# Attention and GELU layer on one core: reordered work between the first softmax and the first output blocks

**Chip, cores, metric.** One core of a Trainium2 chip (trn2). The metric is device time in microseconds (us) of one execution; the span of a profile is some 1.8 us shorter than it.

## The reference

```python
qn = q / (norm(q, axis=1) + 1e-6);  kn = k / (norm(k, axis=1) + 1e-6)   # 4 batches, 6080 x 256
a  = softmax(kn.T @ qn / tau)                                            # 256 x 256 per batch
x  = (v @ a).reshape(24320, 256)
h  = x @ w_in;  out = gelu_tanh(h) @ w_out                               # 256 -> 2048 -> 256
```

The kernel folds `a @ w_in` into one matrix `aw` per batch (256 x 2048), so that a block of 512 rows of v needs only two large products: `hp = aw.T @ v.T`, a gelu on ScalarE (ACT), and `yp = g.T @ w_out`.

## The kernel before

For batch 0, q and k come in ten chunks; each is cast (DVE), squared (ACT), and put into the Gram matrix G and the column sums (TensorE, "PE"). Then comes the softmax of batch 0, then 48 v blocks, in whose gaps the next batch's Gram matrix is computed. SyncE (SP) issues plain stores and DMA transposes; GpSimd (POOL) issues the loads that cast to bf16.

```python
# last chunks of batch 0: q squared by DVE, k by ACT
if n >= n_chunks - 2:
    nc.scalar.activation(sqb[:, 1, lo:hi], st[:, 1, lo:hi], AF.Square)
    nc.vector.tensor_mul(sqb[:, 0, lo:hi], qkb[:, 0, lo:hi], qkb[:, 0, lo:hi])
...
# GpSimd's loads, in this order: first weights in four parts, v block 1, second weights,
# first q/k chunk of batch 1, v block 2
for fs in range(D // 512):
    nc.gpsimd.dma_start(out=win_bf[:, :, fs * 512 : fs * 512 + 512], in_=...)
load_v(1)
for half in range(2):
    nc.gpsimd.dma_start(out=wout_bf[:, half * 8 : half * 8 + 8, :], in_=...)
load_qk(1, 0)
load_v(2)
# softmax of batch 0
nc.scalar.activation(r, cols[:, 0:4], AF.Sqrt)
norms(r)                      # DVE: r + eps, then reciprocal
Gs = scaled(G, r)
keep_clock(5)                 # needless matmuls
T = turned(Gs)                # PE
... exp -> eT; v block 0 turned on PE; row_sums(eT); first products aw = eT.T @ w_in
...
# main loop, per block: DMA transposes of v two blocks ahead, load three blocks ahead
vT = vT_of.pop(nb)
turn_v(nb + 2)                # four dma_start_transpose on SyncE
load_v(nb + 3)
...
# while blocks 0 and 1 run: further loads of batch 1 (n counts the steps)
for n in range(10):
    if n % 5 == 0 and (b, n // 5) not in loaded_of:
        load_qk(b, n // 5)    # the second q/k chunk, at n == 5
    if b == 1 and n == 5:
        turn_v_on_pe(1)
    yield
```

## Time and profile before

| | before |
|---|---|
| time, median of the first 3 runs | 757.6 us (757.37 to 758.07) |
| profiled run | 757.1 us, span 755.3 |
| PE busy | 98% |
| first hp of block 0 / of block 2 | 41.52 us / 67.00 us |
| lost by PE at block 2's first hp | 0.54 us |

The profile's lines are in the prediction. How to read them: after 70 us PE never waits, so the end is set by the moment at which it starts on v block 2. The wait for block 2's turned v just before that is called the door here. Note that the profiled run, 757.1 us, lies at the quick end of the kernel's own spread.

### The profile page before, as it was taken

How to read it: one execution, taken by the hardware profiler on the slowest of the kernel's cores; microseconds unless marked ns; L12 is line 12 of the kernel's file. 1: busy time of each engine (PE TensorE's matmuls, PEld its weight loads, DVE VectorE, ACT ScalarE, POOL GpSimd, SP SyncE). 2: the span in 40 equal slices, each digit the busy share in tenths (PEclk: the TensorE clock that was granted, in tenths of full speed). 3: DMA queues.
4: the chain of work that ended last, by engine and by line, in shares of the span. 5: the costliest groups of instructions: out<-in, count | busy, mean ns of one | idle time of the engine just before them, and what ended most of it. 6: DMA issues, size and time to landing. Idle time of an engine off the chain costs nothing.

```text
span 755.3 us, 12358 instructions
## 1 busy us (share of the span) xinstructions
PE 738.0 (98%) x5272; PEld 504.6 (67%) x5272; DVE 278.3 (37%) x485; ACT 420.3 (56%) x412; POOL 70.0 (9%) x127
## 2 busy tenths in 40 slices
PE   4899999999999999999999999999999999999998
PEld 3556666667666666666666666666767666666666
DVE  3645545454402545553421455454441011011011
ACT  5775555556455555555555555555545655555552
POOL 0231010001021111001031000100101000000000
PEclk9999999999999999999999999999999999999999
DMA  9999957115149678313449385621512633322111
GB/s 351 357 194 180 189 87 154 53 43 83 43 103 214 133 133 137 65 43 66 101 94 221 80 130 101 125 80 47 82 43 78 111 79 76 69 74 53 41 57 56
DMA packets 80759, 83.59 MB, mean 111 GB/s; under 512 B 55488, under 2 KB 60224, under 8 KB 80704
## 3 DMA queue, kind: packets, MB, share of 16 engines
q0 software_dynamic: 17648, 32.97, 27.0%
q1 hardware_dynamic: 62752, 48.98, 24.6%
q8 instruction: 41, 0.67, 0.4%
q10 hardware_dynamic: 304, 0.85, 0.3%
q14 instruction: 14, 0.11, 0.1%
HBM read 78.91 MB, written 24.90 MB: 137 GB/s over the span
## 4 chain that ended last, share of the span: by engine, by line
PE 95%; DMA 3%; DVE 0%; ACT 0%; SPq 0%; issue 0%; DVEq 0%
PE yp L463 44%; PE hp L536 44%; PE G L141 5%; DMA st<-in_k_dram 3%; PE ps L201 2%; PE cols L153 1%; PE T L179 0%; PE yp L567 0%; PE idle L137 0%; SPq L80 0%; DVE qkb L242 0%; ACT g L540 0%; PE ps L348 0%; ACT eT L328 0%; DVE Gs L171 0%
## 5 line engine op out<-in xcount | busy, mean ns | idle before, releaser
L540 ACT ACTIVATE g<-hp 128x1024 bf16<-128x1024 f32 (+1 forms) x384 | 389.8, 1015 | 308.6 <-PE hp L536 308.5
L463 PE MATMUL yp<-wout_bf,g 128*128 128x256 bf16 x3024 | 392.0, 273 | 0.0
L536 PE MATMUL hp<-vT,aw 128*128 128x512 bf16 (+1 forms) x1536 | 390.8, 377 | 0.4 <-ACT g L540 0.4
L463 PEld LDWEIGHTS <-g 128*128 128x128 bf16 x3024 | 295.9, 98 | 113.4
L536 PEld LDWEIGHTS <-aw 128*128 128x128 bf16 x1536 | 149.9, 98 | 105.0 <-issue 1.3
L480 DVE COPY ysb<-yp 128x512 f32<-128x512 f32 (+1 forms) x95 | 64.9, 683 | 403.1 <-PE yp L463 403.1
L404 DVE TENSOR_TENSOR acc<-acc,sq 128x512 f32<-128x512 f32 (+1 forms) x141 | 97.5, 692 | 4.8
L141 PE MATMUL G<-qkb 128*128 128x256 bf16 (+1 forms) x384 | 69.8, 282 | 12.8 <-DVE qkb L242 12.8
L403 DVE TENSOR_TENSOR sq<-qkb 128x512 bf16<-128x512 bf16 (+1 forms) x141 | 58.7, 417 | 0.0
L141 PEld LDWEIGHTS <-qkb 128*128 128x128 bf16 (+1 forms) x384 | 37.8, 101 | 21.5 <-DVE qkb L242 15.0
L280 POOL DMA_DIRECT2D vb<-in_v_dram x47 | 25.5, 544 | 142.7 <-DMA vT<-vb 122.8
L210 DVE TENSOR_SCALAR aw<-ps,rsinv 128x512 bf16<-128x512 f32 x30 | 22.4, 749 | 27.0 <-PE ps L201 26.7
L247 ACT ACTIVATE sqb<-st 128x3072 bf16<-128x3072 f32 (+3 forms) x9 | 20.4, 2287 | 11.6 <-DMA st<-in_k_dram 11.6
L80 POOL DMA_DIRECT2D qkb<-in_q_dram x24 | 13.0, 542 | 148.7 <-PE hp L536 82.4
L242 DVE CAST qkb<-st 128x3072 bf16<-128x3072 f32 (+4 forms) x11 | 14.5, 1326 | 15.4 <-DMA st<-in_k_dram 15.3
L201 PE MATMUL ps<-win_bf,eT 128*128 128x512 bf16 x60 | 17.7, 379 | 0.0
L414 POOL TENSOR_TENSOR r<-r,half 128x4 f32<-128x4 f32 x3 | 3.1, 1044 | 141.7 <-DVE r L413 141.7
L80 POOL DMA_DIRECT2D qkb<-in_k_dram x24 | 13.1, 544 | 4.1 <-DMA qkb<-in_q_dram 2.3
L520 POOL COPY g<-gr 128x1024 bf16<-128x1024 bf16 x2 | 2.1, 1040 | 105.3 <-PE yp L463 105.3
L439 DVE RECIPROCAL den<-den 128x256 f32<-128x256 f32 x6 | 10.5, 1753 | 0.2
L554 POOL COPY gr<-g 128x1024 bf16<-128x1024 bf16 x2 | 2.1, 1036 | 87.6 <-ACT g L540 87.6
L137 PE MATMUL idle<-filler 128*128 128x512 bf16 x36 | 9.5, 391 | 0.0
(65 smaller groups left out, 85.1 us busy)
## 6 DMA issues: line engine op xcount, KB each, us to landing
out_dram<-ysb SPq DMA_DIRECT2D x44, 512.0 KB, 2.9
vb<-in_v_dram POOLq DMA_DIRECT2D x43, 256.0 KB, 8.6
qkb<-in_q_dram POOLq DMA_DIRECT2D x21, 384.0 KB, 6.6
qkb<-in_k_dram POOLq DMA_DIRECT2D x21, 384.0 KB, 8.7
st<-in_q_dram SPq DMA_DIRECT2D x5, 768.0 KB, 9.5
st<-in_k_dram SPq DMA_DIRECT2D x4, 768.0 KB, 11.3
vT<-vb SPq DMA_TRANSPOSE x184, 3.5
out_dram<-ysb SPq DMA_DIRECT2D x4, 384.0 KB, 4.0
```

What stands on the lines that cost most here:

```text
L80: engines[x].dma_start(out=dst[:, x, 0:size, :], in_=src[b, s0 * 128 : (s0 + size) * 128, :].rearrange("(p s) c -> p s c", s=size))
L141: nc.tensor.matmul(G[:, ic, :], lhsT=qk[:rows, 1, s, ic * 128 : ic * 128 + 128], rhs=qk[:rows, 0, s, :], start=first and ic == 0, stop=las ...
L201: nc.tensor.matmul(ps, lhsT=eT[:, jc, ic * 128 : ic * 128 + 128], rhs=win_bf[:, jc, fs * 512 : fs * 512 + 512], start=jc == 0, stop=jc == 1)
L210: nc.vector.tensor_scalar_mul(dst, ps, scale)
L247: nc.scalar.activation(sqb[:rows, :, lo:hi], st[:rows, :, lo:hi], AF.Square)
L280: nc.gpsimd.dma_start(out=t[:, 0:n, :], in_=v_rows[r0 : r0 + n * 128, :].rearrange("(p s) c -> p s c", s=n))
L403: nc.vector.tensor_mul(sq[:rows], flat, flat)
L404: nc.vector.tensor_add(acc[:rows], acc[:rows], sq[:rows])
L463: nc.tensor.matmul(yp[:rows, at, :], lhsT=g[:, fc, s * 128 : s * 128 + rows], rhs=wout_bf[:, fc, :], start=fc == 0, stop=fc == FC - 1)
L480: nc.vector.tensor_copy(ysb[:, s0 : s + 1, :], yp[:, 0 : s + 1 - s0, :])
L536: nc.tensor.matmul(hp[:, j, :cols], lhsT=aw[:, cc, fc * 128 : fc * 128 + 128], rhs=vT[:, cc, :cols], start=cc == 0, stop=cc == 1)
L540: nc.scalar.activation(g[:, 2 * i : 2 * i + 2, :cols], hp[:, :, :cols], AF.Gelu_apprx_tanh)
```

## The change

Its intent: shorten the softmax chain and have v block 2 on the core earlier. The core of the diff:

```diff
-            if n >= n_chunks - 2:
+            if n == n_chunks - 2:            # last chunk: both squares on ACT
...
-    for fs in range(D // 512):
+    for c0, c1 in ((0, 512), (512, 1024), (1024, D)):     # three weight loads
...
+    load_v(2)
     load_qk(1, 0)
-    load_v(2)
...
-    keep_clock(5)
+    (v block 0 turned on PE here: eight transposes into two PSUM tiles)
+    keep_clock(1, pY, "y")
     T = turned(Gs)
+    keep_clock(1, pY, "y")
+    nc.vector.tensor_copy(vT0[:, 0, :], vps[0])
...
+    first_aw(0, 0); first_aw(1, 0)       # products of the first half of eT
     rsinv = row_sums(eT)
+    first_aw(0, 1); first_aw(1, 1); ...  # then of the second half
```

## The prediction

> **What bounds the kernel now.** I read the page first: busy shares, then the chain of work that ended last, to learn which engine's time is the kernel's time.
>
> ```profile
> PE 738.0 (98%) x5272; PEld 504.6 (67%) x5272; DVE 278.3 (37%) x485; ACT 420.3 (56%) x412; POOL 70.0 (9%) x127
> ...
> PE 95%; DMA 3%; DVE 0%; ACT 0%; SPq 0%; issue 0%; DVEq 0%
> ```
>
> TensorE is the kernel: 95% of the chain, 98% busy. A change in another engine's work is worth only the time that it lets TensorE start earlier or wait less. The whole span is 755.3 us and the device time 757.6 us. I then cut the span into stretches, to see where TensorE is not yet full.
>
> ```profile
> 0.00:27.50 27.50, 16.59 (x131) 10.13 (x131) 12.18 (x13) 15.40 (x8) 1.46 (x8) 1.00 0.95 369
> 27.50:36.40 8.90, 6.98 (x106) 5.64 (x107) 7.82 (x9) 7.63 (x5) 3.68 (x6) 1.00 0.97 338
> 36.40:41.60 5.20, 4.63 (x42) 2.96 (x40) 3.30 (x9) 3.53 (x7) 3.93 (x6) 1.00 1.13 153
> ...
> 65.00:70.00 5.00, 4.62 (x30) 2.54 (x29) 3.45 (x7) 2.34 (x3) 2.60 (x5) 1.00 0.87 175
> 70.00:755.00 685.00, 681.75 (x4821) 469.29 (x4819) 241.41 (x433) 374.92 (x373) 54.03 (x96) 1.00 0.47 93
> ```
>
> The columns are stretch, length, busy time of PE, weight loads, DVE, ACT, POOL, then clock, DMA share and GB/s. Up to 36.4 us the kernel waits for the first batch's q and k, which the change does not touch. From 36.4 to 41.6 lies the softmax of the first batch, where filler matmuls inflate the busy time: it is a chain of engines. After 70 us TensorE is full, so whatever is gained before it should reach the end undiminished. One hole is left, in 65 to 70. So the change can act in two places only. The chain in order of time shows the first.
>
> ```profile
> 36.85 0.31 PE cols L153 x8
> ...
> 37.19 0.18 ACT r L320
> ...
> 37.40 0.43 DVE r L164
> ...
> 38.14 0.49 DVE Gs L171
> ...
> 38.77 0.75 PE T L179 x4
> ...
> 39.54 0.85 ACT eT L328 x2
> ...
> 40.44 0.23 PE rs L188 x3
> 40.66 0.90 PE ps L348 x8
> 41.56 1.00 PE hp L536 x4
> ```
>
> Column sums, root, norms, scaled Gram matrix, its turn, two exponentials, row sums, products: 4.7 us with no slack drawn. The turning of v block 0 is not in this list. The chain calls the products (ps) the last link before hp; the timeline of DVE says it less simply:
>
> ```profile
> 39.98 0.69 DVE L337 CAST vT<-vps 128x512 bf16<-128x512 f32 x1 [0.97 <-PE vps L333]
> 40.70 0.17 DVE L194 RECIPROCAL rsinv<-rs 128x2 f32<-128x2 f32 x1
> 40.98 1.28 DVE L357 TENSOR_SCALAR aw<-ps,rsinv 128x256 bf16<-128x256 f32 x3
> ```
>
> The first aw eviction needs the product and the reciprocal. The reciprocal ends at 40.87 and the eviction starts 0.11 us later, the same gap as between the norms' reciprocal (37.85 + 0.19 = 38.04) and Gs (38.14) in the chain. The row sums end at 40.67, so the reciprocal was as early as it could be.
>
> The second place is the hole:
>
> ```profile
> 66.24 0.38 PE L141 MATMUL G<-qkb 128*128 128x256 bf16 x2
> 66.44 0.69 DVE L480 COPY ysb<-yp 128x512 f32<-128x512 f32 x1 [4.21 <-PE yp L463]
> 66.97 0.34 PEld L536 LDWEIGHTS <-aw 128*128 128x128 bf16 x3 [0.63 <-issue]
> 67.00 0.59 PE L536 MATMUL hp<-vT,aw 128*128 128x512 bf16 x2 [0.38 <-ACT g L540]
> ```
>
> Counting eight hp groups per block from 41.5 us, 67.00 is the first hp of v block 2. The profile names a gelu, but this hp reuses the buffer of the gelu that ended at 65.29, and no other block start of the run has that wait. What is special is block 2's turned v: it comes by DMA transposes that SyncE can issue only once v block 2 has landed (its wait ends at 55.15). The fourth was issued at 59.40; the medians of landing over short stretches put its landing at 7.4 us later, 66.8. Then hp starts. G's two matmuls would have let it start at 66.24 + 2 x 0.11 = 66.46, so the loss is 0.54 us.
>
> **What the Trainium skill says.** (1) "DMA: Bandwidth & Descriptors", section "Issuing engines are not separate DMA queues": transfers of all issuing engines run on the same 16 DMA engines and interleave. The trace agrees: the first transpose, beside the q/k loads, took 8.4 us to land, against a median of 3.5 us over the run. So order within the loads is the only lever. (2) "ScalarE: Activation LUTs", "What ACT_TABLE_LOAD costs": an ACTIVATE with immediates takes 186 ns + 0.833 ns per element, a table load 1283 ns. The trace has 0.61 to 0.63 us at 512 elements (formula 0.61), 1.91 at 2048 (1.89), and 1.28 for the load. (3) "TensorE: Matmul & The Clock Gate", "Part 4: PE-mode transpose": transposes do not count as busy for the clock gate as matmuls do. The trace before has 1.6 us of transposes almost unbroken (38.77 to 40.38) at clock 1.00, so it does not show the danger.
>
> **The change, part by part.**
>
> Last chunk's squares: before, ACT squares k (35.43 to 36.06) while DVE casts (to 36.18) and then squares q (36.32 to 36.74), and the column sums' weight loads wait until 36.80. Now ACT does both in one instruction of 1024 elements: 0.19 + 0.85 = 1.04 us, ending at 36.47. The last Gram matmul starts at 36.58 and holds the array 0.11, so the sums start at about 36.70 instead of 36.80. Gain 0.10 us, on the chain.
>
> v block 0 turned early: eight transposes (about 1.04 us in all) move to 37.0 to 38.1, where four of five fillers go away (4 x 0.215 us). v landed at 28.87 + 7.7 = 36.6, in time. One filler ends by 38.4, before Gs at 38.63. The DVE copy (0.69) falls from 39.0 to 39.7, when DVE was idle. In the kernel before, this work lay beside the exponentials and off the chain: it just missed delaying the reciprocal (40.67 against the row sums' 40.67). Gain 0.
>
> Products at the first exponential: two of eight matmuls (0.22 us) move before the row sums. The first product ends 0.11 us sooner, the second 0.22. But the first eviction is still held by the row sums, the reciprocal and the 0.11 us gap; the second, on ACT, starts about 0.12 us sooner, but hp's second matmul would not run before its first has streamed for 0.215. Gain 0, at most 0.1.
>
> v block 2's load ahead of the chunk: the landings before, as issue plus time to landing, are wout's second half 37.82 + 12.5 = 50.3, the chunk's q 52.0, k 53.5, v block 2 55.1. It moves to right behind wout. 256 KB at the 0.2 MB per us of that stretch is 1.3 us, so it lands near 51.6, 3.5 us earlier. Its transposes follow: the fourth at about 63.3, 3 us before it is wanted. Gain 0.54 us. The chunk lands 1.3 us later, near 55.2; its first Gram matmul is at 57.67. Free.
>
> First weights in three loads, not four: they are in place as before, except that columns 1024 to 1535 now wait for the whole last half. Its landing was 35.65 + 8.2 = 43.85. Its first reader (third group of ps) ran at 44.12 and would now run at 44.0. Free by 0.15 us.
>
> Sum: 0.10 + 0 + 0 + 0.54 = 0.64 us, and 757.6 - 0.64 is 756.96. With half of the possible 0.1 from the products I say 756.9.
>
> **Rivals.** (a) The big weight load becomes the wait: if it lands 0.5 us late, the first 0.1 and more is lost, though an earlier start of POOL's next descriptors (one issue of about 0.75 us fewer) speaks against. The gain from block 2 stays or is merged: 757.3. (b) Block 2's hole was another wait, the named gelu or the buffer; then it stays, and the time is 757.5. Against it: it happens once among 47 starts. (c) The products at the first exponential do help, as the author meant, if the 0.11 us gap is not a cost of the reciprocal but the product's end (40.91): then 0.1 to 0.2 more, 756.7. The two ends lie within 0.01 us of each other, so I cannot tell them apart. (d) With fewer fillers the clock drops: a few microseconds at half speed would be 2 us lost, 759. Against it: the early transposes fill the same stretch, and the longest pause gets shorter, from 0.5 us to about 0.25. (e) The chunk, later by 1.3 us and beside the earlier transposes, stalls the Gram matmuls: slack is 2.4 us, so it needs twice the delay.
>
> **Range and chances.** The three runs before spread over 0.7 us, more than the effect. With 0.64 as the base, (c) below and (a), (b) above: 756.2 to 757.6. A 2% change would be 15 us; nothing in 34 us to 70 us can give that, and nothing after it changes. Within 2%: 0.98.
>
> **What would show it.** In the profile after: column sums of the last chunk starting 0.1 us sooner after its last load; SyncE's first transposes near 51.6 instead of 55.15; no wait at the first hp of block 2; the distance from the end of the exponentials to the first hp unchanged at 1.13 us (39.54 + 0.85 to 41.52), less if (c) holds; the third ps group without a wait. It would be wrong if the load of the first 36 us itself shifts from run to run, as nothing of that is in my sum, or if ps waits for the wide weight load.

## The result, and the profile after

| | before | after |
|---|---|---|
| median (6 runs each, same rounds) | 757.59 us (757.25 to 758.07) | 757.62 us (757.0 to 758.44) |
| profiled run, span | 755.3 us | 755.9 us |
| last chunk's cast starts | 35.44 us | 35.28 us |
| first hp of block 0 | 41.52 us | 40.98 us |
| PE ready for block 2 | 66.46 us | 66.11 us |
| first hp of block 2 | 67.00 us | 67.52 us |

The ratio is 1.0001, with a 95% interval of 0.9988 to 1.0014. Ratios in this text are the mean time of one kernel's fast runs over that of the other's of the same rounds, so not quite the ratio of the medians. No change clear of the noise, where I had forecast 0.7 us less; the median lies 0.02 us outside my range.

The timeline of the changed kernel through the softmax (columns: start, duration, engine, line, operation, names, shapes; in brackets the idle time before and what ended it):

```profile
36.52 0.34 PE L153 MATMUL cols<-ones_bf,sqb 128*128 128x1 bf16 x8
...
36.90 0.17 ACT L319 ACTIVATE r<-cols 128x4 f32<-128x4 f32 x1 [0.58 <-PE cols L153]
...
37.11 0.17 DVE L164 TENSOR_SCALAR r<-r 128x4 f32<-128x4 f32 x1 [1.12 <-ACT r L319]
...
40.16 0.17 DVE L194 RECIPROCAL rsinv<-rs 128x2 f32<-128x2 f32 x1 [1.09 <-PE rs L188]
...
40.44 1.27 DVE L369 TENSOR_SCALAR aw<-ps,rsinv 128x256 bf16<-128x256 f32 x3
...
43.77 0.10 PEld L201 LDWEIGHTS <-eT 128*128 128x128 bf16 x1 [0.31 <-issue]
```

This stage did better than forecast. From the last chunk's cast to hp it takes 40.98 - 35.28 = 5.70 us, where it took 41.52 - 35.44 = 6.08. Of the 0.38 us, 0.13 is the squares (cast to root: 36.90 - 35.28 = 1.62, was 1.75). The other 0.25 is one DVE instruction that adds epsilon to four columns: 0.17 us here and 0.42 before. The rest is the same to 0.01 us: root to hp less that instruction is 4.08 - 0.17 = 3.91 now and 4.33 - 0.42 = 3.91 before. (A further 0.16 us of the earlier hp is only an earlier last load.) The last line shows a new wait: the weight load of the third product group comes 0.31 us after the one before it, once the wide weight load is in. Without a wait that gap is 0.12 us, so PE lost 0.19: from the first hp to this group it took 43.77 - 40.98 = 2.79 us, against 44.12 - 41.52 = 2.60 in the kernel before.

The chain of waits of the changed kernel from 50 to 70 us, in order of time, is the answer to the hole of before:

```profile
51.56 1.30 SPq L294
...
55.47 11.80 DMA vT<-vb
...
67.52 1.02 PE hp L548 x4
```

v block 2 is on the core at 51.54 us (before: 55.13), as forecast, and its transposes are issued from 51.56 to 55.47. But the fourth takes 11.8 us to land, at 67.28, where I had assumed some 7.4. The timeline of PE in the changed kernel at this door:

```profile
65.89 0.38 PE L141 MATMUL G<-qkb 128*128 128x256 bf16 x2
67.52 1.02 PE L548 MATMUL hp<-vT,aw 128*128 128x512 bf16 x4 [1.25 <-DMA vT<-vb]
```

PE could have gone on at 65.89 + 0.22 = 66.11 and loses 1.41 us, against 0.54 before. It arrives 0.35 us sooner (the 0.54 of the first hp, less the 0.19 of the third group) and leaves 0.52 later; the spans differ by 0.6. Why do transposes that were issued 3.6 us earlier land no earlier? The DMA view has the packets of each queue; q0 carries GpSimd's loads, q1 the transposes. First the kernel before, from 59 to 63 and from 64 to 67 us (columns: packets, MB, share of the 16 engines' time; a line of a single DMA has its size and its us to landing):

```profile
q0 software_dynamic: 300, 0.75, 96.0%
q1 hardware_dynamic: 295, 0.07, 13.8%
...
q1 hardware_dynamic: 1742, 0.40, 134.8%
q0 software_dynamic: 25, 0.05, 8.9%
```

Then the changed kernel, from 55 to 64 and from 64 to 68 us:

```profile
q0 software_dynamic: 647, 1.64, 97.5%
q1 hardware_dynamic: 593, 0.14, 12.0%
...
qkb<-in_k_dram POOLq DMA_DIRECT2D x1, 384.0 KB, 11.7
...
q1 hardware_dynamic: 1727, 0.45, 117.6%
q0 software_dynamic: 58, 0.13, 16.1%
```

As long as loads are queued, each queue gets one packet in turn: 295 against 300, 593 against 647. But a load's packet carries 0.75 MB / 300 = 2.5 KB and a transpose's 0.07 / 295 = 0.24 KB. So the transposes crawl at 70 packets per us. When the loads thin out, from about 64 us, they go at several hundred per us. The last load queued beside them (the k half of the third q/k chunk, issued at 54.98, the qkb line above) lands at 66.7; block 2's four transposes land at 60.9, 64.7, 66.9 and 67.3. In the kernel before, that load lands at 65.8 and the four at 63.6, 66.1, 66.4 and 66.8. The landing is set by the end of the load queue, not by the issue. The Trainium skill has this rule, "DMA: Bandwidth & Descriptors", section "Queues, rings and completion order": each DMA engine round-robins between its queue rows at packet granularity. The equal counts agree with it; whether the trace's packets are that page's packets, no run here shows. I had quoted another section of that page and not drawn this conclusion.

### The profile page after: what moved, and what is told of

The parts are those of the page before. It is cut to its first block, busy times and chain, and to the rows that moved or that the text cites. A ratio compares the mean times of both kernels' runs of the same rounds, so it can differ in the third digit from the quotient of the medians.

```text
span 755.9 us, 12264 instructions
## 1 busy us (share of the span) xinstructions
PE 731.4 (97%) x5183; PEld 503.5 (67%) x5269; DVE 277.6 (37%) x484; ACT 420.6 (56%) x412; POOL 69.2 (9%) x126
## 4 chain that ended last, share of the span: by engine, by line
PE 90%; issue 5%; DMA 3%; POOL 1%; SPq 0%; ACT 0%; DVE 0%; POOLq 0%; ACTq 0%
PE yp L475 43%; PE hp L548 41%; PE G L141 4%; DMA vb<-in_v_dram 2%; DMA vT<-vb 2%; PE ps L201 1%; SPq L294 0%; POOL win_bf L309 0%; PE cols L153 0%; PE yp L579 0%; POOL wout_bf L312 0%; PE T L179 0%; ACT g L552 0%; POOL vb L280 0%; POOL filler L117 0%
## 5 line engine op out<-in xcount | busy, mean ns | idle before, releaser
L548 PE MATMUL hp<-vT,aw 128*128 128x512 bf16 (+1 forms) x1457 | 385.0, 377 | 5.4 <-DMA vT<-vb 1.3
L247 ACT ACTIVATE sqb<-st 128x3072 bf16<-128x3072 f32 (+4 forms) x10 | 21.4, 2163 | 11.7 <-DMA st<-in_k_dram 9.3
```

Source lines behind the costliest of these rows:

```text
L247: nc.scalar.activation(sqb[:rows, :, lo:hi], st[:rows, :, lo:hi], AF.Square)
L548: nc.tensor.matmul(hp[:, j, :cols], lhsT=aw[:, cc, fc * 128 : fc * 128 + 128], rhs=vT[:, cc, :cols], start=cc == 0, stop=cc == 1)
```

## Experiments

**Theory (queue).** The door at block 2 opens when GpSimd's loads run dry; nothing that PE or the load order of v block 2 gains before it gets past it. **Rivals.** (1) A transpose simply takes 9 to 12 us on this path. (2) There is no door: PE is the bound from 41 us on. (3) The wide weight load ate the gain. There were twelve experiments, all with correct results, five timed runs each, in three sessions; the kernel before ran in each session (medians 757.26, 757.30, 757.47). All edits move or add work only. All verdicts by the 2% rule are "same"; intervals are given where they matter.

### Holding the loads back

```diff
         for n in range(10):
+            if b == 1 and n == 5:     # reads the four turned slices of block 2, so it waits for them
+                nc.gpsimd.tensor_copy(gate2, vT_of[2][0:1, 0, :])
             if n % 5 == 0 and (b, n // 5) not in loaded_of:
                 load_qk(b, n // 5)
```

> The changed kernel, with one small GpSimd copy that reads the four turned slices of v block 2, put before the load of the second q/k chunk, so that no further q/k load is queued beside these transposes. Queue theory (the transposes get one small packet for each large packet of the software loads and land only when those loads run dry): the fourth transpose lands near 58 instead of 67.3, the wait at block 2's first hp (1.25 us) is gone, and the time falls by about 1.3 us, to 756.3. Rival (a transpose simply takes 9 to 12 us from its issue on this queue, whatever else is queued): the fourth still lands near 67, the wait stays at about 1.2 us, time 757.6.

Measured: 756.23 us median (755.98 to 757.79), ratio to before 0.9988 (0.9976 to 1.0001). The slow one, 757.79, has a mean clock of 0.998 (see the end). The timeline of GpSimd in this kernel shows when the last transpose was in:

```profile
59.57 1.08 POOL L398 COPY gate<-vT 1x512 bf16<-1x512 bf16 x1 [13.71 <-DMA vT<-vb]
```

So 59.4 us rather than 67.3. I had said 58; the fourth was issued at 55.53 and took 3.8 us. PE has no wait at all after 42 us. Rival (1) is out.

The same copy went into the kernel before.

> The same copy in the kernel before, where v block 2 lands at 55.1. Queue theory: its transposes land near 60 to 61, the wait at block 2 (0.54 us lost) is gone, the time falls by 0.5 to 757.1. Rival (fixed latency of a transpose): no change, 757.6, wait 0.4.

Measured: 756.46 us (756.26 to 756.84), ratio 0.9988 (0.9974 to 1.0001), and no wait of PE. With no load beside them the four transposes land 2.3 to 2.9 us after their issue, the last at 61.6:

```profile
61.77 0.93 POOL L386 COPY gate<-vT 1x512 bf16<-1x512 bf16 x1 [15.80 <-DMA vT<-vb]
```

The medians differ by 0.80 us, where the profile before had 0.54 to give; the interval holds both, and no gain as well.

As a dose test, the copy was put one chunk later in the changed kernel (`if b == 1 and n == 0` ahead of `load_qk(b, n + 2)`).

> A dose test: the changed kernel with the same small GpSimd copy one load later, before the third q/k chunk, so that only the second chunk and v block 4 (1.0 MB into SBUF, some 5 us at 0.2 MB per us) are queued beside the transposes of v block 2, in place of 1.8 MB. Queue theory: the software loads run dry near 61.5 and the fourth transpose lands at 62 to 64, between 57.8 or so with the early copy and 67.3 with none; no wait at block 2; time as gate_after, about 756.3. Rival (the transposes' own pace): 67.

Measured: 756.07 us (755.98 to 756.24), ratio 0.9983 (0.9971 to 0.9996). GpSimd's timeline, and PE's at block 2, in this kernel:

```profile
64.02 0.60 POOL L407 COPY gate<-vT 1x512 bf16<-1x512 bf16 x1 [12.38 <-DMA vT<-vb]
```

```profile
66.02 1.03 PE L551 MATMUL hp<-vT,aw 128*128 128x512 bf16 x4
```

The landing moves with the number of loads queued beside the transposes: about 59.4 with none beyond v block 3, 63.8 with the second chunk and v block 4, 67.3 with the third chunk as well. And PE goes through the door at 66.02 without a wait. Holding the loads shows that the loads are what delays the transposes; that they do it by taking turns packet by packet rests on the counts above.

### Is it the order, or the transposes?

```diff
-    load_v(2)
     load_qk(1, 0)
+    load_v(2)
```

> The changed kernel with v block 2's load put back behind the q/k chunk; all else of the change stays. Queue theory: v block 2 lands near 55 again, but its fourth transpose still lands near 67, so the early load is worth nothing: time within 0.3 us of the changed kernel, wait 0.8 to 1.2 us. My prediction's step (load order is worth 0.54 us): 0.54 us slower than the changed kernel.

> The changed kernel itself, unedited, to have its time and trace on the same chip and in the same rounds as the next three. Both theories: 757.6 give or take 0.4, a wait of about 1.2 us at block 2's first hp, and no difference from the kernel before that the rounds can resolve.

Measured in the same rounds: old order 757.71 us (756.46 to 758.02), the changed kernel again 757.91 (757.35 to 758.07), before 757.30. Means 757.47 and 757.85. The 0.38 us between them is within the noise, and of the 0.54 us that my prediction gave to the early load nothing shows: the fourth transpose lands at 67.68 in the old order and at 67.67 in the rerun. In the old order's timeline of PE, block 2 starts at the same time as in the changed kernel's rerun (67.92):

```profile
67.93 1.02 PE L548 MATMUL hp<-vT,aw 128*128 128x512 bf16 x4 [0.97 <-DMA vT<-vb]
```

Its third product group came 0.83 us late by the wide weight load (3.43 us from the first hp, not 2.60), and so took part of the wait off the door.

Next, block 2 turned by PE instead of by DMA:

```diff
                 turn_v_on_pe(1)
+            if b == 1 and n == 9:
+                turn_v_on_pe(2)
...
+            if nb > 0:
                 turn_v(nb + 2)
```

> The changed kernel with v block 2 turned by TensorE (eight transposes and a DVE copy, as block 1 already is) in place of the DMA transposes. Both theories expect the wait at block 2 to go and 0.45 us of TensorE to come in; so 0.8 us less than the changed kernel, 756.8. If it stays at 757.6, the hole was not the transposes'.

Measured: median 756.52 us; four runs 756.44 to 756.66 and one at 758.21 with clock 0.998; ratio 0.9993 (0.9980 to 1.0005). No wait at block 2. The hole was the transposes'. It costs PE's eight transposes, and is still no worse than gate_before.

### Does the door swallow work?

```diff
+            if b == 1 and n == 8:
+                pad = pA.tile([128, 512], FP32, tag="a", name="pad")
+                for _ in range(4):
+                    nc.tensor.matmul(pad, lhsT=filler[:, 0:128], rhs=filler, start=True, stop=True)
```

> The changed kernel with four needless matmuls of 512 columns (0.86 us of TensorE) in block 1, ahead of the wait. Queue theory: the landing of v block 2 does not depend on TensorE, so the work is absorbed: the wait shrinks from 1.25 to about 0.4 us, block 2 starts at the same time, and the kernel takes the same 757.6. Rival (TensorE is the bound all along from 41 us, the wait is no barrier): 0.86 us longer, 758.5.

Measured: 758.44 us (758.12 to 758.80). Three of five runs had a mean clock of 0.998, the profiled one among them, so this run could not tell. The two others, 758.12 and 758.43, spoke for the rival.

> The padded kernel (0.86 us of needless matmuls in block 1) once more, because the profile of its first run had 3 us of half clock at 30 us, which hid the question. Queue theory: with an unthrottled profile, block 2's first hp starts at the same distance after the last software load landed as in the unpadded kernel; wait about 0.4 us; time within 0.3 us of the unpadded kernel in these rounds. Rival (no barrier): 0.86 us above it. The first run's times (758.1 to 758.8) lean to the rival, so this is open.

Measured: 756.84 to 758.37, median 758.24, mean 757.83; the unpadded kernel in the same rounds 757.35 to 758.07, median 757.91, mean 757.85. So the 0.86 us of added work shows as -0.02 us in the means and 0.33 in the medians, with a standard error of about 0.35: times of five runs can barely tell 0 from 0.86. In the profile the padded PE arrives at 67.11 and starts block 2 at 67.26, while the unpadded one starts it at 67.92. From the start of the last chunk's cast to the end of the span the padded profile takes 755.6 - 35.59 = 720.0 us and the unpadded one 756.3 - 35.53 = 720.8: with more work it is not longer. But the landing itself varies by most of a microsecond (67.0 to 67.8 in the profiles with the loads not held) and was early in the padded one, at 67.01. So I call the absorption supported, not settled by this pair alone; the first padded runs leaned the other way.

### The wide weight load

> The changed kernel with the first weights in four loads again. Both theories expect the wait of the third product group (0.31 us) to go, as its columns land 1 to 2 us sooner. Queue theory: the 0.3 us comes back as a longer wait at block 2 and the time stays 757.6. Rival (the wide weight load is what ate the gain): 757.3 and a visible step.

The edit: `((0, 512), (512, 1024), (1024, 1536), (1536, D))`. Measured: 757.89 us (757.48 to 758.15). The wait of the third group is gone, and the wait at block 2 is 1.61 us instead of 1.25. But hp of block 0 started late, at 41.32, because the epsilon instruction took 0.51 us, so PE reached the door at 66.04 + 0.22 = 66.26, no sooner than the changed kernel (66.11), and this run could not tell. What answers rival (3) is the trace of the changed kernel: the wide load took 0.19 us of PE's lead of 0.54, and the other 0.35 was still there at the door. Two more runs followed, with the door open.

> gate_after with the first weights in four loads. With no barrier at block 2, gains before it should reach the end. The wait of the third product group (0 to 0.3 us in the runs so far) goes, but GpSimd's issues shift and the norms' first DVE instruction may take 0.4 to 0.5 us in place of 0.17. So 756.0 to 756.5; if both cancel, equal to gate_after.

Measured: 756.53 us (756.30 to 756.95), not better than gate_after. In its timeline the epsilon instruction lies in GpSimd's issue of the second weights and ends with the first of the two (36.89 + 0.90 = 37.79):

```profile
36.89 1.78 POOL L313 DMA_DIRECT2D wout_bf<-in_moe_w_out_dram  x2
37.27 0.52 DVE L165 TENSOR_SCALAR r<-r 128x4 f32<-128x4 f32 x1 [1.11 <-ACT r L320]
```

Then GpSimd was made to wait for the norms ahead of that issue; the root and norms were moved up in the program for it:

```diff
     load_v(1)
+    (r, norms, Gs here)
+    nc.gpsimd.tensor_copy(gate[:, 2:3], r[0:1, 0:1])
     for half in range(2): ... second weights
```

> gate_win4 with GpSimd held at a one-element copy of the norms before it issues the second weights, so that it writes no descriptors while DVE adds the epsilon. Port theory (that DVE instruction waits for GpSimd's issue to end): it takes 0.16 us, and the distance from the root on ACT to the first hp is 4.08 us, not 4.33 to 4.42. Rival (its length is chance): 0.4 or more can show up. Time 0.25 us below gate_win4.

```profile
37.27 0.17 DVE L165 TENSOR_SCALAR r<-r 128x4 f32<-128x4 f32 x1 [1.11 <-ACT r L313]
...
37.84 1.76 POOL L319 DMA_DIRECT2D wout_bf<-in_moe_w_out_dram  x2
```

Measured: median 756.18 us, four runs 756.07 to 756.26, one at 758.38 with clock 0.998. Same start, 37.27, and 0.17 us instead of 0.52; the root to hp distance is 4.09 instead of 4.43; the span falls from 754.7 to 754.4. The medians differ by 0.35 us too, but the means of all five runs do not (756.60 and 756.58), because of the one at 758.38. This agrees with the Trainium skill, "SBUF — State Buffer", section "Who interferes with whom": a DVE `tensor_scalar` in a two-port mode and GpSimd exclude each other, and whoever comes second waits. Not every load issue holds the add up, though (see the last section).

One measure takes the start of the last load, which shifts from 35.27 to 35.89 us between the profiles, out of the comparison: the span less the start of the last chunk's cast. Over the profiles without a half-clock stretch it gives:

| | us |
|---|---|
| door open, epsilon instruction 0.17 us (gate_after, gate_late_after, hold_gate_win4, best) | 718.9 to 719.0 |
| door open, epsilon instruction 0.42 or 0.52 us (gate_before, gate_win4) | 719.3 |
| the kernel before | 719.9 |
| the change with the loads not held, unpadded (after, after_again, oldorder_after, win4_after) | 720.6 to 721.1 |

So a gain in the softmax does reach the end once the door is open: there the change is worth some 0.3 us. And the door cost some 0.6 us in the profile of the kernel before and 1.6 in that of the changed one, the third group's 0.19 included.

### The combination, and the clock

> hold_gate_win4 with six more filler matmuls while TensorE waits for the sixth chunk near 27.5 us (2 us idle there). Twice a profile showed 3 us of half clock from 30 us on, which cost 1.2 to 1.7 us. If that idle stretch is the cause, no run is at a mean clock of 0.998 and the spread of the five runs is under 0.5 us; the fastest run is no faster than hold_gate_win4's. Rival: the half clock comes back in one of five.

The edit: `fillers = [0, 0, 5, 5, 6, 13, 4, 3, 1, 0]` (seven became 13). Measured: 756.21 us (755.88 to 756.30), ratio 0.9984 (0.9971 to 0.9998). It and gate_late_after are the two whose interval lies below 1: about 0.17% below the kernel before. (That of pad_after, 1.0002 to 1.0027, lies above 1.) Neither is shown to be quicker than the other; gate_late_after needs only the copy.

The reason for trying fillers was the profile of the padded kernel, in stretches (the third number from the end of a line is the granted clock):

```profile
27.50:29.50 2.00, 0.00 (x1) 0.01 (x1) 1.82 (x2) 1.81 (x1) 0.00 (x0) 1.00 1.02 406
29.50:33.20 3.70, 3.70 (x27) 2.35 (x28) 3.20 (x4) 3.10 (x3) 0.40 (x2) 0.56 1.05 398
```

After 2 us with no matmul the clock was half for about 3 us; the root on ACT then came at 38.68 instead of about 37.15. Two of the twelve experiments' profiles show it (pad_after and peturn_after), and single runs of the kernel before (758.44) and of others carry the same mark, a mean clock of 0.998. The mark is not exact: one run of after_again has 0.997 at 757.91, its own median. Nor is the gap the whole cause: PE idled 2.02 and 1.98 us in those two profiles, and 2.05 in gate_late_after's, whose clock stayed full. No run of the version with fillers has it, but neither has gate_late_after, which has no more of them than the kernel before. Whether the fillers prevent it stays open.

## Why the prediction was wrong

Point by point, by its own steps:

- **Last chunk's squares, gain 0.10:** right; 0.13 us measured (1.61 to 1.65 from cast to root in all the unthrottled profiles with the change).
- **v block 0 turned early, gain 0, and products at the first exponential, gain 0, at most 0.1:** right. Root to hp without the epsilon instruction is 3.91 us in both kernels, and from the end of the exponentials to hp it is 1.14 us for the 1.13 of before. Rival (c) is out: the reciprocal's path holds the first eviction.
- **Not in the sum:** the epsilon instruction, 0.25 us shorter after the change. I read its 0.42 us in the chain and did not ask why four columns take so long, though the same line takes 0.16 us in the later batches. It ended with GpSimd's load issue (37.40 + 0.42 and 36.92 + 0.91, both near 37.83), as in the runs above. With four weight loads in the changed kernel it took 0.51 us again, so the three loads moved it; nobody had aimed at that, and the gain is luck.
- **Weights in three loads, free by 0.15 us:** not safe. The third group came 0.19 us late in the profile after and 0.83 in the old order's, and not at all in the six other profiles with three loads. Rival (a) was real, but small.
- **v block 2's load ahead, gain 0.54 us: the step that failed.** Its first half held: the block landed at 51.54 for the forecast 51.6. Its second, "Its transposes follow: the fourth at about 63.3", did not. It landed at 67.28, and PE's wait grew from 0.54 us to 1.41. I carried over a landing time of some 7 us as if it belonged to a transpose; it belonged to the queue beside it. Coming earlier means more time spent beside the loads, one small packet to each large one, and the same end. The evidence was in the trace before: landing times of 8.4, 9.6, 8.3 and 7.4 us for issues from 55.15 to 59.40, so landings bunched up after 63 us while the issues were spread. That order within the loads was the only lever was wrong for the same reason: holding later loads back was another.
- **"Whatever is gained before it should reach the end undiminished":** false in the stretch from 41 to 66 us. The door opens at a time set by DMA, so the 0.35 us by which PE came earlier became waiting. That is where the real gain in the softmax went: not off the path, but given back at the next wait.

What put the change at plus 0.03 rather than at minus 0.1 is not settled: the landing varies more from run to run than the two kernels differ. In the profiles the last load landed 0.9 us later after the change (66.7 for 65.8), though it was issued only 0.4 later (54.98 for 54.57). That the longer overlap with the transposes is what delays it is argued only.

## What to carry to other kernels

A small-packet transfer that shares the engines with large loads can land only when the loads end, as the DMA transposes here did; issuing it sooner then does not help, but holding the later loads back behind it by one tiny dependent copy can. Before summing gains along the path of a busy engine, look for the next wait that is timed by something else: everything gained ahead of it can be swallowed, and that wait has to be removed first. When a tiny instruction is long in one place and short in another, ask which lock it met.

## What the Trainium skill lacked or had wrong

- "DMA: Bandwidth & Descriptors", "Queues, rings and completion order": the round robin by packet is there, but not what follows for a DMA transpose, whose tile of 256 B the page gives only in another section. Measured: packets of 0.24 KB beside 2.5 KB, one for one, so the transposes get under a tenth of the bytes; block 2's land 7.4 to 12.7 us after issue beside loads (profiles before and after) and 2.3 to 2.9 us without.
- "SBUF — State Buffer", "Who interferes with whom": the shared pair is said to be held for the whole instruction. Here a DVE add that started 0.10 to 0.22 us into a GpSimd load issue was not held (0.17 us, seven profiles), one that started 0.25 to 0.48 us into it was held to its end (0.32 to 0.52 us, five profiles). That load issues take the lock only in their later part would fit; no run tested it.
- "TensorE: Matmul & The Clock Gate", "Why this matters for your kernels": it advises against idle gaps above about 3 us. Here gaps of 2.02 and 1.98 us were followed by about 3 us at half clock (pad_after, peturn_after), and one of 2.05 us was not (gate_late_after).
